# Copying two parts of a weight on chip by GpSimd in the backward pass of a dense GELU layer

## The chip, the cores and the metric

The kernel runs on one core of one Trainium2 chip. The metric is the device time of one execution in microseconds (us). The kernel before the change takes 264.65 us (median of three runs, 264.45 to 264.73).

## What is computed

A dense layer with a tanh-approximated GELU, and its gradients. Shapes: x and grad_out 2048 x 448 (S x D), w1 448 x 1792 (D x F), w2 1792 x 448, all bf16.

```
u    = x @ w1 + b1              gh  = (grad_out @ w2.T) * gelu'(u)
h    = gelu(u)                  gx  = gh @ w1.T
out  = h @ w2 + b2              gw1 = x.T @ gh      gb1 = sum over rows of gh
                                gw2 = h.T @ grad_out   gb2 = sum over rows of grad_out
```

The six outputs are out, gx, gw1, gb1, gw2 and gb2.

## The kernel before

**Tiling.** The 2048 rows are four blocks of 512, the 1792 columns of F seven pairs of 128-column tiles. A pair of tiles in a block is one of 28 "pairs" p, numbered 7 x block + pair. For each pair, PE computes u (`u`) into two PSUM banks; ScalarE and VectorE copy it out with b1 added (`c`), ScalarE makes the GELU (`g`), a square (`s`) and a tanh (`t`), VectorE the rest of the derivative (`e r y z m n`). PE computes grad_out @ w2.T for the pair (`q`) into banks 6 and 7, and VectorE multiplies it with the derivative (`G`). Products `o` (or `p`, in pieces of two tiles, for the first block) sum out over the tiles, `x` sums gx. `vo` and `vx` copy these sums out of PSUM.

**Halves of the array.** D = 448 is 3.5 times 128. The depth is therefore cut into seven pieces of 64 rows, and PE multiplies two at a time, one in the upper and one in the lower half of the array, each into its own bank. Such a pair of matmuls is a slot. An order of slots comes in two runs (`.1` and `.2` in the names) in which the halves have changed banks. Where a run goes on in a bank that the other half has used before, `run` (from line 227) lets a word travel: a nop on GpSimd's queue (line 236, `word = nc.gpsimd.nop()`) waits for the last matmul of the run before, and the first matmul of the new run waits for that nop.

**Where w1 lies.** `w1_sb` has 128 partitions and four columns of blocks. Blocks 0 to 2 hold the first 384 rows of w1, loaded in four parts of columns (`L0` to `L3`, `LW1`). Block 3 holds the last 64 rows in its partitions 0 to 63 (`R`, `LW1R`) and once more the first 64 rows in its partitions 64 to 127 (`F`, `LW1F`). The first seven pairs don't use block 3: for them the last 128 rows lie in another tile, `w1z`, loaded in three parts (`Z0` to `Z2`, `LW1Z`). From pair 7 on the runs read block 3.

**Other loads.** `K0` to `K3` load w2 in parts, `xr` rows of x, which PE turns with an identity (`X0` to `X3` in PE's order) for the first block. `X`, `Y`, `J` and `I` on SyncE's queue are loads turned by the DMA: x, grad_out, w2 and w1. `Nx` and `Ng` load x and grad_out in rows for the last two loops.

**What sets the order.** Each engine has a list written out by hand: `PE_ORDER`, `ACT_ORDER`, `DVE_ORDER`, `SP_ORDER` (from line 91); GpSimd's is filled by the calls of `pl.op("POOL", ...)` in their order in the text (lines 670 to 672: three entries of memsets). Nothing is reordered on an engine. `Plan.emit` (line 69) walks the five lists in the order PE, ACT, DVE, SP, POOL, and puts out entries of each as long as all that an entry needs has been put out; then it starts the next pass. The words of `run` are put out from inside PE's entries, and so stand in GpSimd's queue at the place that this walk gives them. The program uses eight DMA semaphores in turn, so that a load can wait for the landing of the one eight places before it.

**The end.** After the 28 pairs come the two loops for gw1 (matmuls of line 781) and gw2 (line 835), 16 matmuls a tile. The last tile of gw2 is cut in two pieces, copied out at line 840 and 841 and stored.

Of the kernel before, what the change touches and what calls it, by code (L numbers as in the profile page):

```python
# [88 lines left out]


PE_ORDER = """
W6 X0 X1 w4 X2 X3 h0.1 B h0.2 h1.1 u1.1 h1.2 u1.2 u2.1 u3.1 u2.2 u3.2 p0.0 p0.1 p0.2 p0.3 p1.0 p1.1 u4.1 u5.1 u4.2 u5.2
p1.2 p1.3 p2.0 p2.1 p2.2 p2.3 u6.1 p3.0 u6.2 p3.1 p3.2 p3.3 p4.0 p4.1 u7.1 p4.2 u7.2 p4.3 p5.0 p5.1 p5.2 p5.3 u8.1
p6.0 u8.2 q0.1 p6.1 q0.2 u9.1 p6.2 u9.2 q1.1 p6.3 q1.2 u10.1 o1.0.0.6.1 u10.2 q2.1 o1.1.0.6.1 u11.1 q2.2 u11.2
o1.0.0.6.2 o1.1.0.6.2 q3.1 u12.1 q3.2 u12.2 o1.0.6.10.1 q4.1 o1.1.6.10.1 u13.1 q4.2 u13.2 o1.0.6.10.2 q5.1 o1.1.6.10.2
q5.2 o1.0.10.14.1 o1.1.10.14.1 o1.0.10.14.2 q6.1 o1.1.10.14.2 q6.2 x0.0.0.6.1 x0.1.0.6.1 u14.1 q7.1 u14.2 q7.2
x0.0.0.6.2 x0.1.0.6.2 u15.1 q8.1 u15.2 q8.2 x0.0.6.10.1 x0.1.6.10.1 u16.1 q9.1 u16.2 q9.2 x0.0.6.10.2 u17.1
x0.1.6.10.2 u17.2 q10.1 x0.0.10.14.1 q10.2 u18.1 x0.1.10.14.1 u18.2 q11.1 x0.0.10.14.2 q11.2 u19.1 x0.1.10.14.2 u19.2
q12.1 o2.0.0.6.1 u20.1 q12.2 u20.2 o2.1.0.6.1 o2.0.0.6.2 q13.1 o2.1.0.6.2 q13.2 o2.0.6.10.1 o2.1.6.10.1 q14.1
o2.0.6.10.2 q14.2 o2.1.6.10.2 o2.0.10.14.1 u21.1 q15.1 u21.2 q15.2 o2.1.10.14.1 o2.0.10.14.2 u22.1 q16.1 u22.2 q16.2  # L100
o2.1.10.14.2 u23.1 x1.0.0.6.1 u23.2 x1.1.0.6.1 q17.1 u24.1 q17.2 u24.2 x1.0.0.6.2 q18.1 x1.1.0.6.2 q18.2 x1.0.6.10.1
x1.1.6.10.1 q19.1 x1.0.6.10.2 q19.2 x1.1.6.10.2 x1.0.10.14.1 x1.1.10.14.1 u25.1 q20.1 u25.2 q20.2 x1.0.10.14.2
x1.1.10.14.2 q21.1 u26.1 q21.2 u26.2 x2.0.0.6.1 x2.1.0.6.1 x2.0.0.6.2 u27.1 x2.1.0.6.2 u27.2 q22.1 x2.0.6.10.1 q22.2
x2.1.6.10.1 x2.0.6.10.2 x2.1.6.10.2 q23.1 x2.0.10.14.1 q23.2 x2.1.10.14.1 x2.0.10.14.2 x2.1.10.14.2 q24.1 o3.0.0.6.1
q24.2 o3.1.0.6.1 o3.0.0.6.2 o3.1.0.6.2 q25.1 o3.0.6.10.1 q25.2 o3.1.6.10.1 o3.0.6.10.2 o3.1.6.10.2 q26.1 o3.0.10.14.1
q26.2 o3.1.10.14.1 o3.0.10.14.2 o3.1.10.14.2 q27.1 x3.0.0.6.1 q27.2 x3.1.0.6.1 x3.0.0.6.2 x3.1.0.6.2 x3.0.6.10.1
x3.1.6.10.1 x3.0.6.10.2 x3.1.6.10.2 x3.0.10.14.1 x3.1.10.14.1 x3.0.10.14.2 x3.1.10.14.2
# [12 lines left out]
m6 e7 n6 r7 y7 z7 G5 m7 e8 vo1.0 r8 vo1.1 vo1.2 vo1.3 z8 G6 n7 e9 y8 r9 y9 z9 m8 G7 n8 m9 e10 n9 r10 y10 z10 G8 e11  # L120
r11 m10 z11 n10 y11 G9 e12 r12 m11 z12 n11 y12 G10 e13 m12 r13 n12 z13 vx0.0 vx0.1 G11 vx0.3 e14 y13 r14 y14 z14 m13
n13 m14 G12 n14 e15 r15 y15 z15 G13 m15 e16 n15 r16 y16 z16 G14 m16 e17 n16 r17 y17 z17 G15 vo2.0 vo2.1 m17 e18 n17
r18 y18 z18 vo2.2 vo2.3 G16 m18 e19 n18 r19 y19 z19 G17 m19 e20 n19 r20 y20 z20 G18 m20 e21 n20 r21 y21 z21 G19 e22
r22 m21 z22 n21 y22 G20 vx1.0 vx1.2 e23 r23 y23 m22 z23 G21 m23 n22 n23 e24 r24 y24 z24 m24 n24 G22 e25 r25 y25 z25
# [36 lines left out]
def make_plan(tc, ctx, x, w1, b1, w2, b2, grad_out, out_0, out_1, out_2, out_3, out_4, out_5):  # L161
    nc = tc.nc
    P = 128
    _, S, D = x.shape
# [506 lines left out]
    pl.op("POOL", "b1z", lambda: nc.gpsimd.memset(b1n[:], 0.0), [], ["b1z"], ("tiny", 1))  # L671
    pl.op("POOL", "b2z", lambda: nc.gpsimd.memset(stage[NST - 1][0:64, 0, :], 0.0), [], ["b2z"], ("tiny", 1))

    def b1_turn():
        for i in range(4):
            nc.vector.transpose(out=b1T[32 * i:32 * i + 32, :], in_=b1n[:, 32 * i:32 * i + 32])
# [34 lines left out]
                step[k](int(a))  # L711

    def rows_nat(tag, dst, src, held):
        for s0, s1 in (((0, 8), (8, 16)) if tag == "xn" else ((0, 6), (6, 11), (11, 16))):
            o = pl.op("SP", f"{tag}{s0}", lambda s0=s0, s1=s1: nc.sync.dma_start(
                out=dst[:, s0:s1, :], in_=src[s0 * P:s1 * P, :].rearrange("(s p) d -> p s d", p=P)), [], [tag], ("dma", (s1 - s0) * P * D * 2, "plain"))
# [111 lines left out]
    for ft in range(NF):  # L828
        halves = [(0, D)] if ft < NF - 1 else [(0, D - P), (D - P, D)]
        for (d0, d1) in halves:  # L830
            bk = next_bank()

            def mm(ft=ft, bk=bk, d0=d0, d1=d1):
                for st in range(NS):
                    nc.tensor.matmul(bk_(bk)[:, 0:d1 - d0], lhsT=h_nat[ft][:, st, :], rhs=g_nat[:, st, d0:d1],  # L835
                                     start=(st == 0), stop=(st == NS - 1))
# [3 lines left out]
            fn = (lambda dst=dst, src=src: nc.scalar.copy(out=dst, in_=src)) if eng == "ACT" else \  # L840
                 (lambda dst=dst, src=src: nc.vector.tensor_copy(out=dst, in_=src))  # L841
# [37 lines left out]
```

## Time and profile before

| | |
|---|---|
| median of three runs | 264.65 us |
| profiled execution, its own time | 265.37 us |
| its span, first to last instruction | 263.6 us |
| PE busy | 259.7 us, 99% |
| DVE busy | 200.6 us, 76% |
| ACT busy | 127.1 us, 48% |
| POOL busy | 14.6 us, 6% |
| share of 16 DMA engines in queue 1 | 80.0% |

PE is TensorE's matmul, PEld its weight load, DVE VectorE, ACT ScalarE, POOL GpSimd, SP SyncE. Names with a q behind (SPq, POOLq) are the instructions of that engine's sequencer, such as issues of DMAs and words. In the timeline a row has start and length in us, the engine, the line, the operation, output <- input and the count of instructions drawn together; behind it, in brackets, the idle time ahead of it and what ended it. The busy time of PE is modelled from the instructions' sizes, so that a busy PE need not be at its peak.

### The profile page before, as it was taken

The page shows a single profiled execution, that of the slowest core. Times are in us where ns is not written, and L with a number is a line of the kernel's source. Part 1 is how long each engine was busy: PE and PEld are TensorE (multiplying, and loading weights), DVE is VectorE, ACT ScalarE, POOL GpSimd, SP SyncE. Part 2 cuts the span into 40 slices and gives each one's busy share as a digit, 9 for nine tenths or more (in the row PEclk, how much of TensorE's full clock was granted, in tenths as well). Part 3 has the DMA queues.
Part 4 walks back from the last instruction along what each step waited for, and adds up shares of the span by engine and source line. Part 5 has one row for each costly group of instructions (what it writes and reads, how often), then busy time and mean ns, then how long its engine had stood idle before and what let it go on. Part 6 is the DMA issues. An engine that isn't in the chain of part 4 may idle for free.

```text
span 263.6 us, 5352 instructions
## 1 busy us (share of the span) xinstructions
PE 259.7 (99%) x2185; PEld 157.4 (60%) x2185; DVE 200.6 (76%) x288; ACT 127.1 (48%) x163; POOL 14.6 (6%) x12
## 2 busy tenths in 40 slices
...
PEclk9999999999999999999999999999999999999999
...
GB/s 194 283 148 227 200 154 140 211 349 239 257 216 235 225 215 68 159 216 60 82 226 218 254 43 59 266 194 105 161 227 158 162 196 182 163 200 185 70 72 35
DMA packets 120107, 46.50 MB, mean 176 GB/s; under 512 B 96671, under 2 KB 119953, under 8 KB 120082
## 3 DMA queue, kind: packets, MB, share of 16 engines
q1 hardware_dynamic: 119392, 45.71, 80.0%
...
q8 instruction: 17, 0.28, 0.4%
q14 instruction: 8, 0.07, 0.1%
...
## 4 chain that ended last, share of the span: by engine, by line
PE 90%; SPq 5%; DMA 3%; issue 0%; ACTq 0%; ACT 0%
PE bank L241 42%; PE bank L781 16%; PE bank L835 16%; PE qb L241 16%; SPq L529 4%; DMA w_sb<-in_w_dram 2%; DMA w1f<-in_w_dram 1%; SPq L517 1%; ACTq L517 0%; ACT w_sb L840 0%
## 5 line engine op out<-in xcount | busy, mean ns | idle before, releaser
L241 PEld LDWEIGHTS <-HG 64*128 64x128 bf16 x896 | 59.6, 94 | 28.9 <-POOLq L236 1.5
L241 PE MATMUL qb<-gT,w2Tf 64*128 64x512 bf16 x392 | 53.5, 376 | 0.0
L241 PE MATMUL bank<-w_sb,HG 64*128 64x448 bf16 x448 | 49.1, 349 | 0.3 <-DMA w_sb<-in_w_dram 0.2
L241 PE MATMUL bank<-xT,w1f 64*128 64x512 bf16 (+1 forms) x360 | 48.1, 370 | 0.0
L241 PE MATMUL bank<-w1T_sb,HG 64*128 64x448 bf16 x448 | 47.5, 349 | 0.0
L476 DVE SCALAR_TENSOR_TENSOR HG<-TR,qb 128x1024 bf16<-128x1024 bf16 x28 | 34.1, 1216 | 12.7 <-PE qb L241 12.6
L835 PE MATMUL bank<-w2Tf,HG 128*128 128x448 bf16 (+2 forms) x240 | 42.6, 340 | 0.0
L781 PE MATMUL bank<-w1f,gh_nat 128*128 128x448 bf16 x224 | 42.5, 353 | 0.0
L241 PEld LDWEIGHTS <-w2Tf 64*128 64x128 bf16 x392 | 26.0, 94 | 14.7 <-POOLq L236 0.3
L835 PEld LDWEIGHTS <-HG 128*128 128x128 bf16 x240 | 22.9, 98 | 19.8
L781 PEld LDWEIGHTS <-gh_nat 128*128 128x128 bf16 x224 | 21.8, 98 | 20.6 <-issue 0.4
L241 PEld LDWEIGHTS <-w1f 64*128 64x128 bf16 x382 | 23.5, 94 | 16.2 <-POOLq L236 1.0
L461 ACT ACTIVATE TR<-TR 128x1024 bf16<-128x1024 bf16 x28 | 29.1, 1052 | 6.6 <-DVE TR L451 6.6
L804 DVE TENSOR_TENSOR w1T_sb<-w1T_sb,gh_nat 128x1792 f32<-128x1792 f32 x14 | 28.4, 2026 | 0.5
L786 ACT ACTIVATE TR<-bank 128x448 bf16<-128x448 f32 x14 | 7.6, 543 | 34.9 <-PE bank L781 34.9
L841 DVE CAST w_sb<-bank 128x448 bf16<-128x448 f32 x6 | 3.7, 623 | 25.9 <-PE bank L835 25.9
L840 ACT CAST w_sb<-bank 128x448 bf16<-128x448 f32 (+2 forms) x9 | 4.4, 491 | 37.7 <-PE bank L835 37.7
L810 POOL PARTITION_ALL_REDUCE w1T_sb<-w1T_sb x1 | 10.6, 10568 | 206.9 <-DVE w1T_sb L808 206.9
L436 ACT ACTIVATE TR<-gh_nat 128x1024 bf16<-128x1024 bf16 x15 | 15.7, 1051 | 11.6 <-DVE TR L471 11.6
L466 DVE TENSOR_SCALAR TR<-TR 128x2048 bf16<-128x2048 bf16 x28 | 19.1, 687 | 1.9 <-ACT TR L461 1.7
L471 DVE TENSOR_TENSOR TR<-TR 128x1024 bf16<-128x1024 bf16 x28 | 19.0, 684 | 0.1
L456 DVE TENSOR_TENSOR TR<-TR,HG 128x1024 bf16<-128x1024 bf16 x28 | 19.1, 682 | 0.0
...
## 6 DMA issues: line engine op xcount, KB each, us to landing
...
out_dram<-st SPq DMA_DIRECT2D x16, 224.0 KB, 2.3
...
out_dram<-xT SPq DMA_DIRECT2D x2, 384.0 KB, 3.3
...
```

The source lines that it names most:

```text
L241: m = nc.tensor.matmul(bk_(b)[:, 0:n], lhsT=l, rhs=r, start=st, stop=sp, skip_group_check=True)
L436: pl.op("ACT", f"s{p}", lambda: nc.scalar.activation(out=TR[p % NTR][:, 1], in_=ubuf(p), func=ACT.Square, scale=sc), [("ub", p)], [v], ("a ...
L456: pl.op("DVE", f"R{p}", lambda: nc.vector.tensor_tensor(out=t[:, 1], in0=t[:, 1], in1=hblk(p), op=ALU.mult), [("r", p), ("h", p)], [val((" ...
L461: pl.op("ACT", f"t{p}", lambda: nc.scalar.activation(out=t[:, 0], in_=t[:, 0], func=ACT.Tanh), [("y", p)], [val(("t", p), ("TR0", p % NTR) ...
L466: pl.op("DVE", f"m{p}", lambda: nc.vector.tensor_scalar(out=t[:], in0=t[:], scalar1=1.0, scalar2=None, op0=ALU.subtract), [("t", p), ("r2" ...
L471: pl.op("DVE", f"n{p}", lambda: nc.vector.tensor_tensor(out=t[:, 0], in0=t[:, 0], in1=t[:, 1], op=ALU.mult), [("m0", p), ("m1", p)], [val( ...
L476: pl.op("DVE", f"G{p}", lambda: nc.vector.scalar_tensor_tensor(out=ghblk(p), in0=t[:, 0], scalar=2.0, in1=qb[:, :, :], op0=ALU.subtract, o ...
L529: pl.op("SP", name, lambda: nc.sync.dma_start_transpose(out=dst[:, :, 0:m], in_=rows_of(src, r0 * D, m)), [], v, ("dma", m * 1024, "turn"))
L781: nc.tensor.matmul(bk_(bk)[:, 0:D], lhsT=gh_nat[:, st // 4, ft, st % 4, :], rhs=x_nat[:, st, :], start=(st == 0), stop=(st == NS - 1))
L804: nc.vector.tensor_tensor(out=hs3, in0=a, in1=gh_nat[:, st // 4, :, st % 4, :], op=ALU.add)
L810: pl.op("POOL", "gb1", lambda: nc.gpsimd.partition_all_reduce(gb1_w, hsum, channels=P, reduce_op=bass_isa.ReduceOp.add), ["hsc"], ["gb1"], ...
L835: nc.tensor.matmul(bk_(bk)[:, 0:d1 - d0], lhsT=h_nat[ft][:, st, :], rhs=g_nat[:, st, d0:d1], start=(st == 0), stop=(st == NS - 1))
```

## The change

`LW1R` and `LW1F`, the two loads of block 3 of `w1_sb`, are gone. GpSimd makes both parts instead: F from the first 64 partitions of block 0, R from partitions 64 to 127 of `w1z`. They are put into GpSimd's list behind the three entries of memsets. `Z1` is issued by ScalarE ahead of its table, no longer by SyncE. SyncE's order has the loads of w1 first, then those of w2 with Z2, and then the turned loads. grad_out's rows for the last loop come in five loads. The last copy of gw2 is done by VectorE. The orders of PE, ACT and DVE are written anew; nine copies of gx out of PSUM move from DVE to ACT.

```diff
 PE_ORDER = """
-W6 X0 X1 w4 X2 X3 h0.1 B h0.2 h1.1 u1.1 h1.2 u1.2 u2.1 u3.1 u2.2 u3.2 p0.0 p0.1 p0.2 p0.3 p1.0 p1.1 u4.1 u5.1 u4.2 u5.2
+W6 X0 X1 w4 X2 X3 h0.1 B h0.2 h1.1 u1.1 h1.2 u1.2 u2.1 u3.1 u2.2 u3.2 p0.0 p0.1 p0.2 p0.3 u4.1 u5.1 u4.2 u5.2 p1.0 p1.1
...
 ACT_ORDER = """
-xr12 L0 Z0 b2 table X1 X3 c0A0 c0A1 s0 g0 s1 g1 c2B t0 s2 g2 g3 s3 c5B g4 t1 t2 c6B g5 g6 s4 s5 g7 c8A c8B g8 c9A c9B
+xr12 L0 Z0 b2 Z1 table X1 X3 c0A0 c0A1 s0 g0 s1 g1 c2B t0 s2 g2 g3 s3 c5B g4 g5 t1 c6B t2 g6 s4 s5 g7 c8A c8B g8 c9A
...
-g24 s24 c25A c25B vx1.1 vx1.3 t22 g25 t23 c26A c26B g26 s25 s26 t24 c27A c27B g27 s27 t25 vx2.0 vx2.2 t26 t27 vx3.0
-vx3.2
+t20 s23 c24A c24B t21 vx1.0 vx1.1 g24 s24 c25A c25B t22 vx1.2 t23 vx1.3 c26A s25 c26B g25 s26 t24 g26 c27A c27B s27
+g27 t25 vx2.0 vx2.1 vx2.2 vx2.3 t26 t27 vx3.0 vx3.1 vx3.2 vx3.3
...
 SP_ORDER = """
-xr01 xr24 b1 L1 Z1 L2 K0 L3 K1 F Z2 K2 X1 K3 R Y0 J0 J1 J2 Y1 I0 E J3 I1 So0.1 So0.0 X2 H0 H1 H2 H3 H4 H5 H6 H7 H8 H9
+xr01 xr24 b1 L1 L2 L3 K0 Z2 K2 K1 K3 X1 J1 Y0 J0 J2 I0 E J3 I1 Y1 So0.1 So0.0 X2 H0 H1 H2 H3 H4 H5 H6 H7 H8 H9 T0 T1
...
-    def LW1R(eng="SP"):
-
-        dma(eng, "w1r", w1_sb[0:64, 3, :], w1[MAIN:D, :], [], ["w1r"], F * 128)
-
-    def LW1F(eng="SP"):
-
-        dma(eng, "w1f", w1_sb[64:128, 3, :], w1[0:64, :], [], ["w1f"], F * 128)
+    def CW1(which):
+
+        if which == "R":
+            out, src, rd, v = w1_sb[0:64, 3, :], w1z[64:128, :], [("w1z", i) for i in range(len(REST_COLS))], "w1r"
+        else:
+            out, src, rd, v = w1_sb[64:128, 3, :], w1_sb[0:64, 0, :], [("w1", i) for i in range(len(W1_COLS))], "w1f"
+        pl.op("POOL", v, lambda: nc.gpsimd.tensor_copy(out=out, in_=src), rd, [v], ("rest", F))
...
     pl.op("POOL", "b2z", lambda: nc.gpsimd.memset(stage[NST - 1][0:64, 0, :], 0.0), [], ["b2z"], ("tiny", 1))
+
+    CW1("F")
+    CW1("R")
...
-        for s0, s1 in (((0, 8), (8, 16)) if tag == "xn" else ((0, 6), (6, 11), (11, 16))):
+        for s0, s1 in (((0, 8), (8, 16)) if tag == "xn" else ((0, 4), (4, 7), (7, 10), (10, 13), (13, 16))):
...
-            eng = "DVE" if (ft % 2 == 1 and ft < NF - 1) else "ACT"
+            eng = "DVE" if (ft % 2 == 1 and ft < NF - 1) or (ft == NF - 1 and d0 > 0) else "ACT"
```

More of the change, by code (lines that the diff above doesn't have):

```diff
@@ L91 @@
 PE_ORDER = """
-W6 X0 X1 w4 X2 X3 h0.1 B h0.2 h1.1 u1.1 h1.2 u1.2 u2.1 u3.1 u2.2 u3.2 p0.0 p0.1 p0.2 p0.3 p1.0 p1.1 u4.1 u5.1 u4.2 u5.2
[L93 to L106, printed above, removed]
@@ L107 @@
-x3.1.6.10.1 x3.0.6.10.2 x3.1.6.10.2 x3.0.10.14.1 x3.1.10.14.1 x3.0.10.14.2 x3.1.10.14.2
+W6 X0 X1 w4 X2 X3 h0.1 B h0.2 h1.1 u1.1 h1.2 u1.2 u2.1 u3.1 u2.2 u3.2 p0.0 p0.1 p0.2 p0.3 u4.1 u5.1 u4.2 u5.2 p1.0 p1.1
+p1.2 p1.3 p2.0 p2.1 p2.2 u6.1 p2.3 u6.2 p3.0 p3.1 p3.2 p3.3 p4.0 u7.1 p4.1 u7.2 p4.2 p4.3 p5.0 p5.1 p5.2 u8.1 q0.1
+u8.2 q0.2 p5.3 p6.0 u9.1 p6.1 u9.2 q1.1 p6.2 q1.2 u10.1 p6.3 u10.2 q2.1 o1.1.0.6.1 u11.1 q2.2 u11.2 o1.0.0.6.1
+o1.1.0.6.2 u12.1 q3.1 u12.2 q3.2 o1.0.0.6.2 u13.1 q4.1 u13.2 q4.2 o1.0.6.10.1 o1.1.6.10.1 q5.1 o1.0.6.10.2 q5.2
@@ new lines @@
+o1.1.6.10.2 o1.0.10.14.1 o1.1.10.14.1 q6.1 o1.0.10.14.2 q6.2 o1.1.10.14.2 x0.0.0.6.1 u14.1 x0.0.0.6.2 u14.2 x0.1.0.6.1
+q7.1 x0.1.0.6.2 u15.1 q7.2 u15.2 x0.0.6.10.1 x0.1.6.10.1 q8.1 u16.1 q8.2 u16.2 x0.0.6.10.2 q9.1 x0.1.6.10.2 u17.1 q9.2
+u17.2 x0.0.10.14.1 q10.1 x0.1.10.14.1 u18.1 q10.2 u18.2 x0.0.10.14.2 q11.1 x0.1.10.14.2 u19.1 q11.2 u19.2 o2.0.0.6.1
+q12.1 u20.1 q12.2 u20.2 o2.1.0.6.1 q13.1 o2.0.0.6.2 q13.2 o2.1.0.6.2 o2.0.6.10.1 q14.1 o2.1.6.10.1 q14.2 o2.0.6.10.2
+o2.1.6.10.2 o2.0.10.14.1 u21.1 q15.1 u21.2 q15.2 o2.1.10.14.1 o2.0.10.14.2 u22.1 q16.1 u22.2 q16.2 o2.1.10.14.2 u23.1
@@ new lines @@
+x1.0.0.6.1 u23.2 q17.1 x1.1.0.6.1 u24.1 q17.2 u24.2 x1.0.0.6.2 x1.1.0.6.2 q18.1 x1.0.6.10.1 q18.2 x1.1.6.10.1
+x1.0.6.10.2 q19.1 x1.1.6.10.2 q19.2 x1.0.10.14.1 x1.1.10.14.1 x1.0.10.14.2 u25.1 q20.1 u25.2 q20.2 x1.1.10.14.2
+x2.0.0.6.1 u26.1 q21.1 u26.2 q21.2 x2.1.0.6.1 x2.0.0.6.2 u27.1 x2.1.0.6.2 u27.2 q22.1 x2.0.6.10.1 q22.2 x2.1.6.10.1
+x2.0.6.10.2 x2.1.6.10.2 q23.1 x2.0.10.14.1 q23.2 x2.1.10.14.1 x2.0.10.14.2 x2.1.10.14.2 q24.1 o3.0.0.6.1 q24.2
+o3.1.0.6.1 o3.0.0.6.2 o3.1.0.6.2 q25.1 o3.0.6.10.1 q25.2 o3.1.6.10.1 o3.0.6.10.2 o3.1.6.10.2 q26.1 o3.0.10.14.1 q26.2
@@ L108 @@
+o3.1.10.14.1 o3.0.10.14.2 o3.1.10.14.2 q27.1 x3.0.0.6.1 q27.2 x3.1.0.6.1 x3.0.0.6.2 x3.1.0.6.2 x3.0.6.10.1 x3.1.6.10.1
+x3.0.6.10.2 x3.1.6.10.2 x3.0.10.14.1 x3.1.10.14.1 x3.0.10.14.2 x3.1.10.14.2
 """
 ACT_ORDER = """
-xr12 L0 Z0 b2 table X1 X3 c0A0 c0A1 s0 g0 s1 g1 c2B t0 s2 g2 g3 s3 c5B g4 t1 t2 c6B g5 g6 s4 s5 g7 c8A c8B g8 c9A c9B
-g9 c10A c10B t3 t4 g10 s6 c11A c11B s7 g11 t5 c12A c12B g12 s8 t6 c13A c13B g13 s9 t7 s10 t8 c14A c14B t9 g14 s11 s12
-c15A c15B t10 g15 c16A c16B s13 t11 g16 c17A c17B s14 t12 g17 c18A c18B s15 g18 vx0.2 c19A c19B t13 t14 g19 s16 c20A
@@ L113 @@
-c20B s17 g20 t15 s18 t16 s19 c21A c21B t17 g21 c22A c22B s20 t18 g22 c23A c23B g23 s21 t19 s22 t20 s23 c24A c24B t21
-g24 s24 c25A c25B vx1.1 vx1.3 t22 g25 t23 c26A c26B g26 s25 s26 t24 c27A c27B g27 s27 t25 vx2.0 vx2.2 t26 t27 vx3.0
-vx3.2
+xr12 L0 Z0 b2 Z1 table X1 X3 c0A0 c0A1 s0 g0 s1 g1 c2B t0 s2 g2 g3 s3 c5B g4 g5 t1 c6B t2 g6 s4 s5 g7 c8A c8B g8 c9A
+c9B t3 g9 c10A c10B g10 s6 t4 c11A c11B g11 s7 t5 c12A c12B g12 s8 c13A c13B t6 g13 s9 t7 t8 s10 s11 c14A c14B t9 g14
+s12 c15A c15B g15 t10 c16A c16B g16 s13 t11 c17A c17B g17 s14 t12 c18A c18B vx0.0 vx0.1 s15 t13 vx0.2 c19A c19B vx0.3
@@ L116 @@
+g18 s16 t14 c20A c20B g19 s17 g20 t15 s18 t16 s19 c21A c21B t17 g21 c22A c22B g22 s20 c23A c23B t18 t19 g23 s21 s22
+t20 s23 c24A c24B t21 vx1.0 vx1.1 g24 s24 c25A c25B t22 vx1.2 t23 vx1.3 c26A s25 c26B g25 s26 t24 g26 c27A c27B s27
+g27 t25 vx2.0 vx2.1 vx2.2 vx2.3 t26 t27 vx3.0 vx3.1 vx3.2 vx3.3
 """
 DVE_ORDER = """
-ident X0 X2 b1T c0B0 b2c c0B1 c1A c1B e0 r0 y0 c2A c3A c3B z0 e1 m0 r1 n0 z1 c4A c5A c4B e2 y1 r2 y2 z2 c6A m1 m2 n1 n2
-c7A c7B Dg0 G0 vo0.2 vo0.3 e3 r3 vo0.0 vo0.1 z3 G1 y3 e4 r4 y4 z4 m3 n3 m4 G2 n4 e5 r5 y5 z5 G3 m5 e6 n5 r6 y6 z6 G4
@@ L120 @@
[L120 to L124, printed above, removed]
@@ L125 @@
-m25 G23 n25 vx2.1 vx2.3 e26 r26 y26 z26 G24 m26 e27 n26 r27 y27 z27 m27 n27 G25 G26 vo3.0 vo3.1 vo3.2 vo3.3 G27 vx3.1
-vx3.3
+ident X0 X2 b1T c0B0 b2c c0B1 c1A c1B e0 r0 y0 c2A c3A c3B z0 e1 m0 r1 n0 c4A c5A c4B z1 e2 y1 r2 y2 z2 c6A m1 n1 m2 n2
+c7A c7B Dg0 G0 e3 r3 y3 z3 vo0.2 vo0.3 G1 m3 vo0.0 vo0.1 n3 e4 r4 y4 z4 G2 m4 e5 n4 r5 y5 z5 m5 G3 n5 e6 r6 y6 z6 G4
+e7 m6 r7 n6 z7 G5 y7 e8 r8 y8 m7 vo1.0 vo1.1 z8 vo1.2 m8 vo1.3 n7 n8 G6 e9 r9 y9 z9 m9 n9 G7 e10 r10 y10 z10 G8 m10
+e11 n10 r11 y11 z11 G9 m11 e12 n11 r12 y12 z12 G10 m12 e13 n12 r13 y13 z13 G11 m13 e14 n13 r14 y14 z14 G12 e15 m14 r15
@@ L127 @@
+n14 z15 y15 G13 e16 r16 m15 z16 n15 y16 G14 e17 m16 r17 n16 z17 y17 G15 e18 vo2.0 m17 r18 vo2.1 z18 n17 G16 vo2.2
+vo2.3 e19 y18 r19 y19 z19 m18 n18 m19 G17 n19 e20 r20 y20 z20 G18 m20 e21 n20 r21 y21 z21 G19 e22 r22 m21 z22 n21 y22
+G20 e23 r23 y23 m22 z23 n22 m23 G21 n23 e24 r24 y24 z24 m24 n24 G22 e25 r25 y25 z25 m25 G23 n25 e26 r26 y26 z26 m26
+G24 n26 e27 r27 y27 z27 m27 n27 G25 G26 vo3.0 vo3.1 vo3.2 vo3.3 G27
 """
 SP_ORDER = """
-xr01 xr24 b1 L1 Z1 L2 K0 L3 K1 F Z2 K2 X1 K3 R Y0 J0 J1 J2 Y1 I0 E J3 I1 So0.1 So0.0 X2 H0 H1 H2 H3 H4 H5 H6 H7 H8 H9
```

8 lines of the change are left out of this document (3 added, 5 removed).

## The prediction

> **What bounds the kernel now.** I read the profile's first and second part, then the chain that ended last, then the first 14 us of the timeline, and last the landing times of the loads.
>
> ```profile
> span 263.6 us, 5352 instructions
> ...
> PE 259.7 (99%) x2185; PEld 157.4 (60%) x2185; DVE 200.6 (76%) x288; ACT 127.1 (48%) x163; POOL 14.6 (6%) x12
> ...
> PEclk9999999999999999999999999999999999999999
> ```
> ```profile
> 44.46 0.65 PE qb L241 x6
> ...
> 176.05 42.48 PE bank L781 x224
> 218.53 42.43 PE bank L835 x240
> 260.95 0.02 issue
> 260.98 0.27 ACT w_sb L840
> ```
>
> TensorE is the bound: busy 99%, and from 23 us on the chain is nothing but PE rows. Ideal lengths come from the same rows: six half-height matmuls of 512 columns, three slots, take 0.65 us, 0.216 a slot; 224 of 448 columns take 42.48, 0.190 each. The 392 slots of u and q (28 blocks, 7 each) and the 448 slots and 448 full matmuls of the rest make 392 x 0.216 + 896 x 0.190 = 254.9 us. PE's first real product starts at 5.17 and the last ends at 260.95: 255.8. So nearly 1 us is all that better orders or earlier loads can win once PE runs; the rest is the 5.2 us ahead and 2.7 behind. A change that stops PE, on the other hand, is paid in full.
>
> ```profile
> 0.72 0.49 POOL L668 MEMSET st<- 32x1 f32 x4 [0.29 <-POOLq L863]
> ...
> 1.14 0.15 PEld L367 LDWEIGHTS <-const-bfloat16-1.0 128*128 128x128 bf16 x1 [0.27 <-issue]
> ...
> 1.26 0.19 POOL L671 MEMSET b1n<- 32x128 bf16 x1
> ...
> 1.41 0.47 POOL L672 MEMSET st<- 64x448 bf16 x1
> ...
> 1.57 0.15 PEld L367 LDWEIGHTS <-const-bfloat16-1.0 128*128 128x128 bf16 x1 [0.28 <-issue]
> ...
> 2.78 1.28 ACT L709 ACT_TABLE_LOAD   x1 [2.78 <-POOL st L672]
> ...
> 3.37 0.34 SPq L517 DMA_DIRECT2D gh_nat<-in_w_dram  x1
> ...
> 4.05 0.47 PEld L367 LDWEIGHTS <-const-bfloat16-1.0 128*128 128x128 bf16 x4
> ...
> 4.47 0.58 PEld L576 LDWEIGHTS <-TR 128*128 128x128 bf16 x8
> ...
> 5.17 0.50 PE L241 MATMUL bank<-xT,w1f 64*128 64x256 bf16 x6
> ...
> 5.89 0.22 PEld L241 LDWEIGHTS <-w1f 64*128 64x128 bf16 x5 [0.29 <-POOLq L236]
> ...
> 8.84 0.33 PEld L241 LDWEIGHTS <-w1f 64*128 64x128 bf16 x6 [0.67 <-DMA w1f<-in_w_dram]
> ...
> 11.87 2.38 PE L241 MATMUL bank<-w_sb,HG 64*128 64x448 bf16 x20
> ```
> ```profile
> L236 POOLq EVENT_SEMAPHORE  x112: 17/17/17, 5.8 to 174.6; - x112
> ```
> ```profile
> PEld L241 <- POOLq L236: 2.8, 16, 0.3
> ```
>
> The row at 5.89 is the one to keep. Every time the halves of the array change banks, `run` puts a word on GpSimd's queue (L236) that waits for PE, and PE's next load of weights waits for that word. There are 112 words, the first at 5.8 us, for h0.2, PE's second step on w1. Now a word costs PE 0.3 us at most (2.8 us in 16 waits), because behind the memsets nothing else stands on GpSimd's queue until 174.6.
>
> **The change, part by part.** *The two copies.* They are the fourth and fifth entry of GpSimd's list, behind the three memsets. The emitter walks the lists in turn and puts out an entry once all it needs is put out. In its second pass all loads of w1 and w1z are out, so both copies go out in that pass; PE's X0 still lacks the identity, which DVE puts out in that same pass after PE's turn. So both copies stand ahead of all 112 words. Copy F needs every part of w1 landed (L0 to L3), copy R every part of w1z (Z0 to Z2). In the program as built from the kernel before, an instruction carries one wait and its further waits stand ahead of it as instructions of the sequencer. With three loads to wait for in F and two in R, GpSimd's sequencer stops at them, and behind it the word that h0.2 needs. PE runs in order, so behind h0.2 stands everything else: PE stops at 5.9 until the last of w1 and of w1z is in.
>
> When is that? Landings, each counted from the start of its issue:
>
> ```profile
> 3.75 0.43 SPq L517 DMA_DIRECT2D w1f<-in_w_dram  x1
> ...
> 5.20 0.47 SPq L517 DMA_DIRECT2D w1f<-in_w_dram  x1
> 5.71 0.49 SPq L517 DMA_DIRECT2D w_sb<-in_w_dram  x1
> ```
> ```profile
> w1f<-in_w_dram SPq DMA_DIRECT2D x1, 576.0 KB, 7.1
> ...
> w1f<-in_w_dram SPq DMA_DIRECT2D x1, 384.0 KB, 5.0
> ```
> ```profile
> w_sb<-in_w_dram SPq DMA_DIRECT2D x1, 224.0 KB, 7.9
> ```
> ```profile
> 5.00:10.00 5.00, 4.83 (x60) 2.56 (x59) 4.20 (x10) 2.79 (x5) 0.00 (x0) 1.00 0.96 284
> ```
>
> L2 (384 KB) lands at 3.75 + 5.0 = 8.75, L3 (576 KB) at 5.20 + 7.1 = 12.3, K1 at 5.71 + 7.9 = 13.6. By size, in KB and in order of issue: x 448, L0 192, Z0 128, L1 192, Z1 128, L2 384 (sum 1472 when L2 is in), K0 224, L3 576, K1 224 (sum 2496 when K1 is in). That is 1024 KB in 4.86 us, 211 KB/us. In the new order L3 comes ahead of K0, at a sum of 2048: 8.75 + 576/211 = 11.5. Z2 follows L3 and K0, at 2464: 8.75 + 992/211 = 13.45. At the 284 GB/s (277 KB/us) of the 5 to 10 us row instead it is 12.3; with K1's 7.9 us from an issue near 5.8 it is 13.7. I take 13.45, since that rate comes from landings and not from bytes moved. With the word's usual 0.2 us, h0.2 starts at 13.6 instead of 5.89: **+7.7 us**.
>
> The copies' own length is then off PE's path: their results are read first by block 7, far behind. No row shows a GpSimd copy; the nearest, the memset of 448 columns, took 0.47, so 1792 columns take 1.9 us each by it, and a copy that reads as well up to twice that, 3.8. R runs while DVE takes up its work again; should the two hinder each other, PE, then still slow, is the cover: 0, and at most R's 1.9.
>
> *The cold start.* At the start PE's weight loads of the wake matmuls stand 0.43 us apart (1.14, 1.57) for 512 columns, against 0.216 later; four loads take 0.47 at 4.05, 0.12 each, and eight take 0.58 at 4.47, 0.07 each. PE thus runs at half rate from 0.76 to about 4.5, although the granted clock reads full in the page. A pause of 6 to 7 us may bring that back. Ends: nothing, or the same 3.7 us at half rate, a loss of 1.9. No row shows PE after a pause like it. I take the far end rounded, **+1.8**: the start is the only place of the trace where PE comes out of idleness.
> The Trainium skill, TensorE: Matmul & The Clock Gate (Part 1), says that one idle window of about 3.4 us halves the clock and that as much steady work restores it; by it the loss is 1.7. The spacing at the start agrees.
>
> *Z1 on ScalarE's queue*, ahead of the table. On SP it went out at 3.37 after waiting for a part of x; on ACT the table (2.78 to 4.06) slips behind it by about 1 us, and with it X1's copy and h0.1. Cover: the stall. With the cover gone it costs 1.0.
>
> *The loads left out and the new order of loads.* F and R save 448 KB, R behind a turned load. What PE waited for goes: 0.67 us for L2 at 8.84, and parts of the short waits up to 23 us; at most the 0.9 us of slack found above. Two issues off SP ease nothing else while PE stands. The turned loads start behind K3; they must be in for q0, which the stall puts off as well. **-0.7**, ends 0 and -0.9.
>
> *Orders anew.* Same PE instructions. Nine gx evictions move from DVE to ACT:
>
> ```profile
> 60.00:100.00 40.00, 40.00 (x396) 25.80 (x394) 37.91 (x63) 32.20 (x40) 0.00 (x0) 1.00 1.05 227
> 100.00:140.00 40.00, 40.00 (x398) 27.61 (x395) 38.26 (x64) 30.74 (x38) 0.00 (x0) 1.00 0.58 130
> ```
>
> DVE is at 95% in these stretches and ACT at 80%, so it is a relief for DVE, but PE is full in both: 0. If an order misfits, PE shows it as new waits; I leave 0.5 either way for it.
>
> *g_nat in five loads, not three* (SP, just ahead of the last turn of gh), and *the last copy on DVE*:
>
> ```profile
> 165.97 2.10 SPq L715 DMA_DIRECT2D w2Tf<-in_grad_out_dram  x3
> 168.16 5.17 SPq L520 DMA_TRANSPOSE gh_nat<-HG  x1
> ...
> 254.88 0.62 DVE L841 CAST w_sb<-bank 128x448 bf16<-128x448 f32 x1 [5.43 <-PE bank L835]
> ...
> 257.91 0.53 ACT L840 CAST w_sb<-bank 128x448 bf16<-128x448 f32 x1 [5.52 <-PE bank L835]
> ...
> 260.98 0.27 ACT L840 CAST w_sb<-bank 128x128 bf16<-128x128 f32 x1 [0.47 <-PE bank L835]
> ```
>
> Two more issues of 0.7 hold the turn at 168.16 back by 1.4; it ends at 173.3, and its data are needed only by the last products of the L781 loop that starts at 176.05. g_nat itself is needed at 218. 0; with the cover gone, 1.4. The last copy of 128 columns: DVE's 448 take 0.09 more than ACT's, so 0.27 becomes 0.2 to 0.36, and ACT was idle 0.47 ahead of it, so it gains nothing by being free: 0.
>
> *Sum*: 7.7 + 1.8 - 0.7 = +8.8. The profiled execution took 265.37 (span 263.6 and 1.8 around it): 274.2. The median of the runs, 264.65, lies 0.7 lower: **273.4 us**.
>
> **Rivals.**
> *No stall; about the same time.* The words pass GpSimd's copies while these wait. For it: the four memsets at 0.72 were all handed on within 0.49 us, so the queue holds more than one instruction. Against it: of five waits only two ride on the copies. Then the 1.0 of Z1 stands, the 0.67 at 8.84 goes, K0 lands behind L3 (sum 2272: 12.5 us, p0 wants it near 12.2, +0.3), the slack behind gives 0.2 and the tail 0: +0.4, **265.1**, with 264.0 to 265.6 by the orders. It decides if the first word stands near 6 us.
> The Trainium skill, Perfetto Trace Analysis (Per-instruction lifecycle), has it that an engine instruction waits in a wait queue while the sequencer decodes the next one, but a sequencer-only instruction waits in the sequencer; no row of this trace shows such an overtaking.
> *The copies must be finished, too.* GpSimd takes the word only when R is done: 13.45 plus 1.9 to 3.8. For it: the word and copies share a queue; against it: the memsets at 1.26 and 1.41 (0.19 long) overlap. +1.9 to +3.8: **275.3 to 277.2**.
> *A shorter stall.* PE resumes with L3 alone, 11.5, or Z2 lands at 12.3, or the clock stays up: each takes 1.1 to 2.0 off, **271.4 to 272.3**; two of them together 269.8.
>
> **Chances.** Measurement tells 0.2%, 0.5 us, from nothing. The forecast 0.6; copies finished first 0.12; the shorter stall 0.17; no stall 0.11, of which 0.04 faster, 0.04 the same, 0.03 slower. All but these 0.08 is slower: 0.92. The range holds the forecast, the shorter stall and most of the third: 269.6 to 276.6, which leaves out no stall and the upper half of finished copies, 0.17.
>
> **What the profile would show.** Right: in the timeline GpSimd's two copies near 11.5 and 13.5 us; the first L236 word just behind them; PE's row for h0.2 with an idle time of about 6.5 us put down to GpSimd's queue; PE rows of double length for 3 to 4 us behind it, the granted clock perhaps still at 1; then PE dense to the end and the two loops of 42.4 us unchanged. h0.1 starts about 1 us later than 5.17. Wrong: the first word at 6 us with a copy behind it in time; an idle time that ends well before 12 (another load is last); a PE that is as fast behind the pause as ahead of it; or waits of PE in the middle of the kernel that the new orders bring in.

## The result and the profile after

The changed kernel takes 272.52 us (median of six runs, 272.48 to 273.42) against 264.81 us for the kernel before (median of six, 264.45 to 265.1): a ratio of 1.0294, with a 95% interval of 1.0278 to 1.0311. It is 7.7 us slower. Of its six runs four took 272.5 us at a mean granted clock of 0.987 and two 273.4 us at 0.981; by these means the clock was at half for about 7.0 us in the four and 10.3 us in the two (an estimate, 2 x (1 - clock) x span), and the trace that was kept is one of the four. 273.4 was predicted, with a range of 269.6 to 276.6.

The page of the changed kernel:

```profile
span 270.7 us, 5357 instructions
...
PE 262.2 (97%) x2185; PEld 150.5 (56%) x2185; DVE 197.2 (73%) x280; ACT 131.5 (49%) x171; POOL 17.9 (7%) x14
...
PEclk9779999999999999999999999999999999999999
```

The span has grown by 7.1 us; the rest of the 7.7 is that the profiled execution of before lay 0.56 above the median of its six runs. PE's busy time has grown by 2.5 us with the same 2185 matmuls, so the rest of the span's growth is PE standing idle. The granted clock, which read 9 in all 40 slices before, reads 7 in the second and third. Both losses lie within the first 20 us, as the timeline of the changed kernel shows (start, length, engine, line, operation; in brackets the idle time ahead and what ended it):

```profile
5.96 0.54 PE L240 MATMUL bank<-xT,w1f 64*128 64x256 bf16 x6
...
6.43 0.35 PE L652 MATMUL qb<-st,const-bfloat16-1.0 64*128 64x448 bf16 x1
...
10.67 1.67 POOL L609 COPY w1f<-w1f 64x1792 bf16<-64x1792 bf16 x1 [8.80 <-DMA w1f<-in_w_dram]
11.70 0.34 PEld L240 LDWEIGHTS <-w1f 64*128 64x128 bf16 x5 [5.28 <-POOLq L235]
...
12.40 1.67 POOL L609 COPY w1f<-gh_nat 64x1792 bf16<-64x1792 bf16 x1
...
13.60 0.15 PEld L240 LDWEIGHTS <-w1f 64*128 64x128 bf16 x2 [0.27 <-issue]
14.03 0.15 PEld L240 LDWEIGHTS <-gh_nat 64*128 64x128 bf16 x2 [0.27 <-issue]
...
19.59 1.67 PE L240 MATMUL bank<-w_sb,HG 64*128 64x448 bf16 x16
```

PE works from 5.96 to 6.78, and then its next load of weights (h0.2) waits 5.28 us for GpSimd's queue, the word of `run` (line 235 of the changed kernel). It had gone ahead at 5.89 before. The two copies of line 609 stand around the word: F from 10.67, R from 12.40. Behind the pause the weight loads stand 0.43 us apart (13.60, 14.03), as at the cold start. The first products `p0` begin at 19.59 instead of 11.87. The chain of waits of the changed kernel names the steps between (start, length, what):

```profile
5.20 5.25 DMA w1f<-in_w_dram
10.45 0.03 issue
10.47 0.02 POOLq L609
...
10.54 0.04 POOLq L609
...
10.67 0.88 POOL w1f L609
...
11.63 0.03 POOLq L235
11.66 0.05 issue
11.70 5.02 PE bank L240 x34
...
183.10 42.48 PE bank L781 x224
225.58 42.43 PE bank L835 x240
```

L3, issued at 5.20, lands at 10.45; GpSimd's sequencer then passes its instructions of line 609; the word goes at 11.63 and PE at 11.70. The chain draws the step from 10.67 to 11.55 as the copy F, but F itself ends at 12.34, so the word did not wait for its end. The load that was in at that moment is Z2, by its issue in the timeline and its landing in the list of DMAs:

```profile
6.14 0.47 SPq L516 DMA_DIRECT2D gh_nat<-in_w_dram  x1
```
```profile
gh_nat<-in_w_dram SPq DMA_DIRECT2D x1, 192.0 KB, 5.4
```

6.14 + 5.4 = 11.54. The answer for line 609 of the same trace shows who waited for it:

```profile
L609 POOLq EVENT_SEMAPHORE  x3: 17/17/43, 10.5 to 11.5; - x3
```

These are three instructions of the sequencer itself, two for F and one for R, spread from 10.5 to 11.5: the waits that no longer fit on the copies. The last of them ends the pause.

The clock by windows of the changed kernel (from and to, the length, the busy time of PE, PEld, DVE, ACT and POOL, then the granted clock, DMA share, GB/s):

```profile
8.00:9.00 1.00, 0.00 (x0) 0.00 (x0) 0.00 (x0) 0.00 (x0) 0.00 (x0) 1.00 1.02 365
9.00:10.00 1.00, 0.00 (x0) 0.00 (x0) 0.00 (x0) 0.00 (x0) 0.00 (x0) 0.74 1.02 334
10.00:11.00 1.00, 0.00 (x0) 0.00 (x0) 0.00 (x0) 0.00 (x0) 0.33 (x1) 0.50 0.98 315
...
15.00:16.00 1.00, 1.00 (x12) 0.55 (x10) 0.13 (x1) 0.24 (x1) 0.00 (x0) 0.50 1.26 283
16.00:17.00 1.00, 1.00 (x12) 0.39 (x10) 0.59 (x2) 0.79 (x2) 0.00 (x0) 0.84 0.81 172
17.00:18.00 1.00, 1.00 (x12) 0.47 (x10) 1.00 (x2) 1.00 (x2) 0.00 (x0) 1.00 1.06 170
```

A mean of 0.74 between 1.00 and 0.50 puts the fall near 9.5 us; 0.84 puts the return near 16.3 (0.32 of that window at 0.50). PE worked at half rate from 11.70 to there, 4.6 us, in which it did 2.3 us of work.

From 19.59 on nothing is added: `p0` starts 7.7 us later than before, the L781 loop 7.05 later (183.10 against 176.05), and both last loops have their 42.48 and 42.43 us.

### The profile page after: what moved, and what is told of

Same layout as the page of the kernel before. It is cut to its first block, busy times and chain, and to the rows that moved or that the text cites. A ratio compares the mean times of both kernels' runs of the same rounds, so it can differ in the third digit from the quotient of the medians.

```text
span 270.7 us, 5357 instructions
## 1 busy us (share of the span) xinstructions
PE 262.2 (97%) x2185; PEld 150.5 (56%) x2185; DVE 197.2 (73%) x280; ACT 131.5 (49%) x171; POOL 17.9 (7%) x14
## 4 chain that ended last, share of the span: by engine, by line
PE 95%; DMA 3%; POOL 0%; issue 0%; ACTq 0%; DVE 0%; POOLq 0%; DVEq 0%
PE bank L240 47%; PE qb L240 17%; PE bank L781 16%; PE bank L835 16%; DMA w1f<-in_w_dram 3%; POOL w1f L609 0%; ACTq L516 0%; DVE w_sb L841 0%; POOLq L609 0%; POOLq L235 0%; DVEq L841 0%
## 5 line engine op out<-in xcount | busy, mean ns | idle before, releaser
L240 PEld LDWEIGHTS <-HG 64*128 64x128 bf16 x896 | 55.3, 94 | 32.5 <-POOLq L235 1.9
L240 PE MATMUL bank<-xT,w1f 64*128 64x512 bf16 (+1 forms) x360 | 49.6, 383 | 5.0 <-POOLq L235 4.9
L240 PE MATMUL qb<-gT,w2Tf 64*128 64x512 bf16 x392 | 52.9, 376 | 0.0
L240 PE MATMUL bank<-w_sb,HG 64*128 64x448 bf16 x448 | 48.2, 349 | 0.0
L781 PE MATMUL bank<-w1f,gh_nat 128*128 128x448 bf16 x224 | 42.5, 352 | 0.0
L240 PEld LDWEIGHTS <-w1f 64*128 64x128 bf16 x382 | 22.6, 97 | 23.9 <-POOLq L235 6.0
L240 PEld LDWEIGHTS <-w2Tf 64*128 64x128 bf16 x392 | 24.1, 94 | 16.7 <-POOLq L235 0.2
L781 PEld LDWEIGHTS <-gh_nat 128*128 128x128 bf16 x224 | 21.8, 98 | 20.6 <-issue 0.4
L841 DVE CAST w_sb<-bank 128x448 bf16<-128x448 f32 (+1 forms) x7 | 4.0, 577 | 35.2 <-PE bank L835 35.2
L840 ACT CAST w_sb<-bank 128x448 bf16<-128x448 f32 (+1 forms) x8 | 4.2, 519 | 37.2 <-PE bank L835 37.2
L410 ACT ACTIVATE ub<-bank,b1T 128x512 bf16<-128x512 f32 (+1 forms) x22 | 13.6, 660 | 12.1 <-PE bank L240 12.1
```

Of the source, the lines that this page charges most:

```text
L240: m = nc.tensor.matmul(bk_(b)[:, 0:n], lhsT=l, rhs=r, start=st, stop=sp, skip_group_check=True)
L410: fn = lambda: nc.scalar.activation(out=out, in_=src, func=ACT.Identity, bias=bias)
L781: nc.tensor.matmul(bk_(bk)[:, 0:D], lhsT=gh_nat[:, st // 4, ft, st % 4, :], rhs=x_nat[:, st, :], start=(st == 0), stop=(st == NS - 1))
```

## The experiments

Each was run beside the kernel before on the same chip. That kernel's medians on these occasions were 264.86, 264.86 and 264.91 us.

### The loads again, in the new order

```diff
-... K0 Z2 K2 K1 K3 X1 J1 ...
+... K0 Z2 K2 K1 K3 F R X1 J1 ...
...
+    def LW1R(eng="SP"):
...
+    def LW1F(eng="SP"):
...
-    CW1("F")
-    CW1("R")
```

> The changed kernel with the two parts of w1 loaded again (behind K3 on SyncE's queue) in place of the copies, all else as changed. If the copies' place is the cause: no pause, about 265 us, within 0.5 us of the run with the copies put out late. If the rest of the change made the loss: near 272.5 us. It also shows when L3 lands in the new order of loads with PE at work: 10.4 us if the order sets it, about 12 us if PE's standing still did.

Measured: 265.83 us (265.65 to 266.3), ratio 1.0033, interval 1.001 to 1.0056. Its timeline:

```profile
5.74 0.47 SPq L516 DMA_DIRECT2D gh_nat<-in_w_dram  x1
...
5.93 0.65 PE L240 MATMUL bank<-xT,w1f 64*128 64x256 bf16 x6 [0.22 <-ACT xT L582]
...
6.79 0.22 PEld L240 LDWEIGHTS <-w1f 64*128 64x128 bf16 x5 [0.29 <-POOLq L235]
...
12.43 1.68 PE L240 MATMUL bank<-w_sb,HG 64*128 64x448 bf16 x16
```

Without the copies in front the word costs its 0.29 us and the pause is gone. So the two entries in GpSimd's list make 6.7 of the 7.7 us (272.52 against 265.83); the rest of the change is left with about 1.0. The profile splits them: h0.2 starts at 6.79 here and at 11.70 in the changed kernel, 4.9 us of pause. The 0.9 from 5.89 to 6.79 is the later start of h0.1 (5.93 against 5.17) and a little more; most of it is made up again by 176 us, where this kernel's loop for gw1 (line 780 here) starts at 176.18. The landing of L3, which was asked for too, is not in this trace's list of loads; that of Z2 is (5.74 + 5.8 = 11.54). The kernel with the copies put out late, below, is 1.2 us slower than this one, and not within 0.5.

### The changed kernel with PE kept busy in the pause

Twenty more matmuls of ones into a spare bank, whose results nobody reads, stand between h0.1 and h0.2.

```diff
-W6 X0 X1 w4 X2 X3 h0.1 B h0.2 h1.1 ...
+W6 X0 X1 w4 X2 X3 h0.1 B W20 h0.2 h1.1 ...
```

> The changed kernel with 20 more matmuls of 512 columns of ones, whose results nobody reads, on PE between B and h0.2, that is, in the pause. If the pause costs twice, once as a pause and once as a cold clock behind it: the word still comes at 11.6 us, the granted clock stays at 1, and 2.3 us of the 7.7 go: about 270.2 us. If the rows of double length have another cause (the loads or the copies beside them): unchanged, 272.5 us.

Measured: 270.40 us (270.09 to 271.13), ratio 1.0214, interval 1.0192 to 1.0236. Its timeline:

```profile
6.64 4.05 PEld L366 LDWEIGHTS <-const-bfloat16-1.0 128*128 128x128 bf16 x20 [0.29 <-issue]
...
11.69 0.22 PEld L240 LDWEIGHTS <-w1f 64*128 64x128 bf16 x5 [0.99 <-POOLq L235]
...
17.32 1.68 PE L240 MATMUL bank<-w_sb,HG 64*128 64x448 bf16 x16
```

and one of its windows:

```profile
9.00:10.00 1.00, 1.00 (x7) 0.46 (x5) 0.00 (x0) 0.00 (x0) 0.00 (x0) 1.00 1.05 345
```

The word comes when it did, but the granted clock reads 1.00 here and in every other window up to 19 us, behind the word PE is at full rate, and `p0` starts at 17.32, not 19.59. So the clock costs 2.3 us by the traces and 2.1 by the medians, apart from the pause.

### Only F in front, R behind u3

```diff
-        pl.op("POOL", v, ...)
+        o = pl.op("POOL", v, ...)
+        if which == "R":
+            after(o, [("u", 3, 0), ("u", 3, 1)])
```

> The changed kernel with copy F left in front of all words and copy R put out behind block 3's u. If the word is held only by the waits that stand in the queue ahead of it: it comes when L3 has landed, 10.5 us, while copy F still runs, PE's pause is 1.1 us shorter, and the time 271.0 to 271.6 us. If the word also needs the copy in front of it to be done (10.7 + 1.7): it comes at 12.4 us and the time is 273 us or more.

Measured: 273.2 us (272.28 to 274.58), ratio 1.0312, interval 1.0279 to 1.0345. Its timeline:

```profile
11.15 1.67 POOL L609 COPY w1f<-w1f 64x1792 bf16<-64x1792 bf16 x1 [9.28 <-DMA w1f<-in_w_dram]
11.22 0.34 PEld L240 LDWEIGHTS <-w1f 64*128 64x128 bf16 x5 [4.82 <-POOLq L235]
...
18.49 1.80 POOL L609 COPY w1f<-gh_nat 64x1792 bf16<-64x1792 bf16 x1 [5.66 <-PE bank L240]
18.67 2.17 DVE L450 TENSOR_TENSOR TR<-TR,ub 128x1024 bf16<-128x1024 bf16 x1
...
22.27 0.82 PE L240 MATMUL qb<-xT,w1f 64*128 64x512 bf16 x6 [1.22 <-ACT ub L410]
```

The mechanism came out, the time did not. The word goes with the start of F, at 11.2, while F runs until 12.82: a copy that runs holds no word, only a wait that stands in the sequencer does. That ends the rival "the copies must be finished". But the start 0.5 us earlier won PE only 0.2 (`p0` at 19.38 against 19.59). The clock came back near 16.4 us (0.81 in the window from 16 to 17, 0.50 in the one before), no earlier than in the changed kernel, so that the half-rate stretch was longer. And R's copy now ran beside VectorE: an operation of 0.68 us took 2.17 (its row in the changed kernel stands in the next fence), and PE waited 1.22 for what came of it, which is more than was won.

### Both copies later

First behind u5, the rest of the changed kernel untouched:

```diff
-        pl.op("POOL", v, ...)
+        after(pl.op("POOL", v, ...), [("u", 5, 0), ("u", 5, 1)])
```

> The changed kernel with one thing other: the two GpSimd copies are put out only behind block 5's u, so that they stand behind the words of the first blocks in GpSimd's queue. If the place of the copies in that queue is the cause, PE's pause of 4.9 us and the half-rate stretch behind it are gone, the first word stands near 6.6 us and the kernel takes about 265 us (264.0 to 265.8, the rest of the change being worth little). If the other parts (the orders, Z1 on ScalarE, the order of the loads) made the loss, it stays near 272.5 us.

Measured: 267.01 us (266.97 to 267.13), ratio 1.0082, interval 1.0067 to 1.0098. The operations of VectorE in the changed kernel, where no copy runs beside them:

```profile
18.88 0.68 DVE L450 TENSOR_TENSOR TR<-TR,ub 128x1024 bf16<-128x1024 bf16 x1
...
163.66 0.69 DVE L470 TENSOR_TENSOR TR<-TR 128x1024 bf16<-128x1024 bf16 x1
```

and the timeline of this experiment:

```profile
19.43 3.86 POOL L609 COPY w1f<-w1f 64x1792 bf16<-64x1792 bf16 x1 [17.55 <-DMA w2Tf<-in_w_dram]
...
23.35 2.02 POOL L609 COPY w1f<-gh_nat 64x1792 bf16<-64x1792 bf16 x1
23.88 2.05 DVE L470 TENSOR_TENSOR TR<-TR 128x1024 bf16<-128x1024 bf16 x1
...
25.43 0.39 PE L240 MATMUL bank<-xT,w1f 64*128 64x512 bf16 x2 [1.36 <-POOL w1f L609]
```

The pause and the half rate are gone (h0.2 at 6.63), but now the copies are late and long: F takes 3.86 us, VectorE's operation three times its 0.69, and PE waits 1.36 us for R at pair 7, the first that reads block 3. The L781 loop starts at 177.56, 1.5 us later than before. The place in the queue came out as the cause; the time lies above the 265.8 that was the upper end.

Then earlier, behind u3, and with Z1 back on SyncE's queue:

```diff
-xr12 L0 Z0 b2 Z1 table X1 ...
+xr12 L0 Z0 b2 table X1 ...
-xr01 xr24 b1 L1 L2 L3 K0 ...
+xr01 xr24 b1 L1 Z1 L2 L3 K0 ...
-        pl.op("POOL", v, ...)
+        after(pl.op("POOL", v, ...), [("u", 3, 0), ("u", 3, 1)])
```

> The changed kernel with the copies put out behind block 3's u (ahead of p0's words) and Z1 issued by SyncE again, behind L1. With the copies behind block 5's u PE waited 1.9 us at block 7 for them; that wait should be gone (the copies run from about 12 to 18 us). Z1 back should bring h0.1 from 5.9 to about 5.2 us. If Z1 on ScalarE is what the rest of the change costs, 264.6 to 265.0 us; if the orders cost it, about 265.8 us.

Measured: 265.77 us (264.9 to 266.71), ratio 1.003, interval 1.0016 to 1.0044. Its timeline:

```profile
9.09 0.33 PEld L240 LDWEIGHTS <-w1f 64*128 64x128 bf16 x6 [1.05 <-DMA w1f<-in_w_dram]
...
11.33 1.67 POOL L609 COPY w1f<-w1f 64x1792 bf16<-64x1792 bf16 x1 [9.46 <-PE bank L240]
...
13.66 1.61 DVE L455 TENSOR_TENSOR TR<-TR,HG 128x1024 bf16<-128x1024 bf16 x1
```

h0.1 starts at 5.03 again, and what was won there PE waits at 9.09 for L2. Here both copies are short (R takes 1.67 from 13.06) and PE waits for neither, though one operation of VectorE beside R takes 1.61. With the stall and its followers gone, the changed kernel ends 0.3% above the one before. The median is that of the second branch, the orders, while the trace shows the wait for L2; as this trace is of an execution of 265.07 us, it does not hold what makes the median 265.77, and the two are not told apart.

A third one, with the copies behind u3, asked whether Z1 can stay on ScalarE behind the first copy out of PSUM:

```diff
-xr12 L0 Z0 b2 Z1 table X1 X3 ...
+xr12 L0 Z0 b2 table X1 Z1 X3 ...
```

> The changed kernel with the copies behind block 3's u and Z1 issued by ScalarE behind the table and X1's copy. h0.1 starts near 5.2 us as before, L2 goes out ahead of Z1. If ScalarE's wait ahead of its table is what Z1 costs, as good as with Z1 on SyncE, 264.3 to 265.0 us; if the wait for X0's rows or anything else holds h0.1, about 265.8 us.

Measured: 266.39 us (265.85 to 268.39), ratio 1.0066, interval 1.004 to 1.0091. A miss, by one row of its timeline:

```profile
11.44 0.39 PE L240 MATMUL qb<-xT,gh_nat 64*128 64x512 bf16 x2 [2.08 <-DMA gh_nat<-in_w_dram]
```

Z1 then lands too late: PE waits 2.08 us for it.

### The copies in the kernel before

The loads F and R of the kernel before are left out of SyncE's order and the two copies put behind its memsets, all else as before.

```diff
-... K0 L3 K1 F Z2 K2 X1 K3 R Y0 ...
+... K0 L3 K1 Z2 K2 X1 K3 Y0 ...
+    CW1("F")
+    CW1("R")
```

> The kernel before with only the two copies by GpSimd in place of the two loads, at the same place in GpSimd's list; orders, Z1 and the other loads as before. If the place of the copies alone makes the loss: PE stops at 5.9 us until the last of w1 and w1z lands, here later than in the changed kernel since K0 and K1 come first, 12 to 13.5 us, and the kernel takes 272.5 to 274.5 us. If the new orders or Z1 made the loss: about 264.8 us.

Measured: 273.06 us (272.58 to 273.69), ratio 1.0309, interval 1.0282 to 1.0336. Its timeline, its chain of waits and the answer for the line of the copies:

```profile
13.36 0.82 PE L241 MATMUL bank<-xT,w1f 64*128 64x256 bf16 x5 [6.63 <-POOLq L236]
```
```profile
5.33 6.66 DMA w1f<-in_w_dram
```
```profile
L610 POOLq EVENT_SEMAPHORE  x3: 43/43/43, 12.0 to 13.2; - x3
```

The copies alone make the stall; the new orders are not needed for it. With the old order of loads L3 lands at 5.33 + 6.66 = 12.0, the last of the three waits in the sequencer is met at 13.2, and PE resumes at 13.36, 1.7 us later than in the changed kernel. The time is only 0.5 us longer: here too the clock comes back within the window from 16 to 17 (mean 0.88), so PE, resuming later, worked at half rate for less time.

The same with the copies behind u3:

```diff
+        after(pl.op("POOL", v, ...), [("u", 3, 0), ("u", 3, 1)])
```

> The kernel before with only the two copies by GpSimd in place of the two loads, put out behind block 3's u instead of in front. If the place in the queue is all that costs: as fast as before, 264.3 to 265.0 us, since the loads they replace were off PE's path. If the copies beside VectorE's work cost something (3.9 us for one beside VectorE against 1.7 alone): up to 266 us.

Measured: 265.57 us (265.1 to 266.15), ratio 1.0025, interval 1.0014 to 1.0036. No stall, and no gain from 448 KB less to load. It lies 0.7 us above the kernel before, in the second branch of what was expected: an operation of VectorE beside copy R takes 1.91 us in its trace. But h0.1 starts at 5.61 there and not at 5.17, so what makes the 0.7 is not separated.

### Z1's own price, and another cut of w1

The loads again, as in the first experiment, with Z1 back on SyncE as well:

```diff
-xr12 L0 Z0 b2 Z1 table X1 ...
+xr12 L0 Z0 b2 table X1 ...
-xr01 xr24 b1 L1 L2 L3 K0 ...
+xr01 xr24 b1 L1 Z1 L2 L3 K0 ...
```

> The changed kernel with the two parts of w1 loaded again and Z1 issued by SyncE again: what is left of the change are the orders, the order of the other loads, the five loads of grad_out's rows and the last copy on VectorE. Against the run with the loads alone put back (265.8 us) it prices Z1 on ScalarE with the stall gone: if h0.1's later start (5.9 against 5.2 us) counts in full, 264.8 to 265.1 us; if PE then only waits at block 2 for L2 instead, which Z1 on SyncE puts back, 265.6 to 265.9 us.

Measured: 265.23 us (264.83 to 265.98), ratio 1.0019, interval 1.0006 to 1.0032. That lies between the two ranges expected. Against 265.83 this is 0.6 us less, but the two intervals overlap; what the traces show is h0.1 at 5.11 and not at 5.93.

Last, the kernel before with its third part of w1 cut in two, so that PE need not wait 0.67 us at 8.84 for all of L2:

```diff
-    W1_PART = (0, 1, 2, 2, 3, 3, 3)
-    W1_COLS = ((0, 256), (256, 512), (512, 1024), (1024, F))
+    W1_PART = (0, 1, 2, 3, 4, 4, 4)
+    W1_COLS = ((0, 256), (256, 512), (512, 768), (768, 1024), (1024, F))
-xr01 xr24 b1 L1 Z1 L2 K0 L3 K1 F ...
+xr01 xr24 b1 L1 Z1 L2 L3 K0 L4 K1 F ...
```

> The kernel before with L2 cut in two loads of 256 columns, so that block 2 waits for the first of them only. If the 0.67 us that PE waits for L2 at 8.8 us in the kernel before is worth its length, 264.2 to 264.5 us; if the loads behind it or the copies out of PSUM set PE's pace there, 264.8 us or, by the additional issue, 265.2 us.

Measured: 265.57 us (264.73 to 265.95), ratio 1.002, interval 1.0008 to 1.0032. Among its waits:

```profile
PE bank L241 <- DMA w_sb<-in_w_dram: 1.2, 1, 1.2
```

This is a miss, above all that was expected: the wait for L2 is replaced by one of 1.2 us for K0, which now lands later. No version beat the kernel before.

## Why the prediction was right, and where its sizes were off

**The stall: right in mechanism, mis-sized.** +7.7 was predicted, +5.8 measured (h0.2 from 5.89 to 11.70). The step that failed is the rate of 211 KB/us for the landings. L3 was put at 11.5 and landed at 10.45, Z2 at 13.45 and landed at 11.54. The rate came from K1 and L2 of the kernel before, that is, from the old order of loads. In the new order Z2 lands before 13.45 also where PE is at work: at 11.54 in the kernel with the loads again (5.74 issued, 5.8 us to land, the row below), at 11.5 to 12.4 in the six such kernels, with L3 at 10.3 to 11.1 in the four of them that list it. In the three kernels of the old order that list it L3 was in at 11.8 to 12.3, with PE at work or not.

```profile
gh_nat<-in_w_dram SPq DMA_DIRECT2D x1, 192.0 KB, 5.8
```

So the order of loads goes with the earlier landing, not PE's standing still. Why the old order lands later was not tried. One of the signs set down was not met: the first word did not come behind both copies but ahead of R, since R's wait in the sequencer held it and not R itself.

**The cold clock: right in mechanism, a little too small.** +1.8 was taken, near the far end of 0 to 1.9; the runs gave 2.1 and the traces 2.3, above that end. The sentence of the prediction that the column of the granted clock might still read 1 was wrong for this pause: it read 0.50. The Trainium skill, TensorE: Matmul & The Clock Gate (Part 1), gives about 3.4 us of idleness for the fall and as much steady work for the return. That a pause halves the clock agrees; the lengths differ here, 2.7 us from PE's last matmul to the fall (6.78 to 9.5) and 4.6 from its resuming to the return.

**What is recovered: about right.** -0.7 was predicted. The pause of 5.8 and the half rate of 2.3 come to 8.1, and the L781 loop is 7.05 late: -1.05. Most of it is the 0.9 by which h0.2 is late without the pause too, and of which the kernel with the loads again has made up 0.8 at 176.18.

**The sum.** Predicted 7.7 + 1.8 - 0.7 = 8.8; in the profiles 5.8 + 2.3 - 1.05 = 7.05; in the medians 7.7. The prediction's 273.4 is 0.9 above the measured 272.52. That it is no further off, with the stall 1.9 too long, is in part luck: the clock cost 0.5 more than was taken, and the profile of before is of an execution 0.56 above the median, so that the medians lie further apart than the profiles.

**Z1 on ScalarE.** 1.0 predicted for h0.1, 0.8 measured (5.17 to 5.96), and hidden under the stall as said. But the 0.8 is not clean: with Z1 ahead of the table h0.1 starts at 5.87 to 5.96 in all five kernels, with Z1 on SyncE at 5.01 to 5.17 in four, but at 5.61 and 5.90 in the two that put copies into the kernel before. With the cover gone the medians give 0.6 (265.83 against 265.23), and their intervals overlap, so a price is not shown. One reason why it can be less than 1.0: with Z1 on SyncE h0.1 starts earlier, and PE then waits for L2 (1.05 us at 9.09, in the kernel with Z1 back and the copies behind u3).

**The copies' own length.** 1.9 to 3.8 us each was the bound; each took 1.67 while VectorE had little to do, and cost nothing on PE's path, as predicted. That changes where one meets VectorE's work: up to 3.86 us for the copy, and 0.9 to 1.5 us more for one operation of VectorE.

**The rest of the change at 0: within the 0.5 left for it in the profile, not in the medians.** With the loads again, and all the new orders, the loop for gw1 starts only 0.13 us later than before, though the medians stand 1.0 apart (265.83 against 264.86), and behind it the changed kernel adds nothing, with five loads of g_nat and the last copy on VectorE. By the last window of the changed kernel's timeline the last copy takes as long as before, 0.29 against 0.27:

```profile
268.10 0.29 DVE L841 CAST w_sb<-bank 128x128 bf16<-128x128 f32 x1 [5.54 <-PE bank L835]
```

**The rivals.** "The copies must be finished" fell: the word went at 11.63 while F ran to 12.34 and R had not begun. "A shorter stall" is what the sizes came to for Z2's landing, with the clock in full on top. "No stall" fell, though half of its argument held: the word did pass R, which was waiting for its turn in GpSimd's queue until 12.40. The Trainium skill, Perfetto Trace Analysis (Per-instruction lifecycle), has an instruction of the engine wait in a queue of its own while the sequencer goes on, and an instruction of the sequencer wait in the sequencer; the trace agrees with both halves, with R at 12.40 behind the word at 11.63, and with three waits that held that word until 11.5. The sum for "no stall", 265.1, was near what the copies behind u3 gave, 265.77.
